# K leaves PSUM as one plain copy, its masked copies are made from SBUF, and the engine queues are ordered anew (two transformer layers, one core)

## The chip, the cores and the metric

One core of one Trainium2 chip runs the whole program. The engines are TensorE (PE, matmuls), VectorE (DVE), ScalarE (ACT), GpSimd (POOL) and SyncE (SP, which issues the DMAs here). Each works through its own queue in order; semaphores join them. The metric is the device time of one execution in microseconds, the median of several runs.

## The reference

Two times in a row, with the same weights, x becomes x plus attention of the normed x, and then x plus an MLP of the normed x. x has 2048 tokens of 512 features; there are 32 heads of 16; a token sees itself and the 255 tokens before it.

```python
def _layernorm(x, axis=-1, eps=1e-5):
    m = jnp.mean(x, axis=axis, keepdims=True)
    v = jnp.var(x, axis=axis, keepdims=True)
    return (x - m) / jnp.sqrt(v + eps)
...
    def _A_ref(x, wqkv, wo):
        B, S, D = x.shape
        H = 32; Dh = D // H; W = 256
        ...
        scores = jnp.einsum("bhqd,bhkd->bhqk", q, k) * (Dh ** -0.5)
        idx = jnp.arange(S)
        mask = (idx[:, None] - idx[None, :] >= 0) & (idx[:, None] - idx[None, :] < W)
        scores = jnp.where(mask[None, None], scores, -1e9)
        p = _softmax(scores, axis=-1)
        o = jnp.einsum("bhqk,bhkd->bhqd", p, v)
        return (lambda x, *d: x.transpose(*d))(o, 0, 2, 1, 3).reshape(B, S, D) @ wo
    def _B_ref(x, w1, b1, w2, b2):
        h = jnp.einsum("bsd,df->bsf", x, w1) + b1
        h = _gelu(h)
        return jnp.einsum("bsf,fd->bsd", h, w2) + b2
    x = A_x
    x = x + _A_ref(_layernorm(x, axis=-1), A_wqkv, A_wo)
    x = x + _B_ref(_layernorm(x, axis=-1), B_w1, B_b1, B_w2, B_b2)
    x = x + _A_ref(_layernorm(x, axis=-1), A_wqkv, A_wo)
    x = x + _B_ref(_layernorm(x, axis=-1), B_w1, B_b1, B_w2, B_b2)
```

## The kernel before

**Tiling.** x stays in SBUF as 16 tiles of 128 tokens. Attention goes in blocks of 256 tokens, 8 for each of the two layers, so blocks 0 to 15; the MLP goes in ten jobs of two or four tiles (`JOBS`). The program is written as if block followed block (`lnq`, `kv`, `attention`, `mlp`), and every instruction becomes a node of a plan.

**One block.** `layernorm` takes the statistics on DVE (line 618, 620), adds epsilon (L624, on POOL or DVE), raises to -1/2 on POOL (L630), and `transposed` writes the normed row on DVE (L640); a DMA transpose (L645) brings it into the layout for the projections. Only the four first tiles are transposed by PE instead (L652). `lnq` projects Q, two groups for a block, and copies each out of PSUM by `evac` on DVE (L607) or ACT (L609) into a ring `QT` of `QR` blocks. `kv` projects K, two groups, and V, two groups.

**K in two masked copies.** A chunk of 128 features holds 8 heads of 16. The scores of a pair of heads come out of one matmul of 32 rows: K is stored twice, once with the odd heads' rows set to zero and once with the even heads'. `parmask` holds the two columns of ones and zeros. Before, one DVE instruction reads a projection's bank and writes both (L700), broadcasting the bank over the two masks, 1024 elements a partition.

**Scores and PV.** `visit` makes 512 columns of scores in four banks (L767, "score group"), ACT takes exp of two banks at once into `E` (L774, 300 of them), masks of the window's edges are multiplied in place on DVE or POOL (L795). `pv` multiplies with V (L819, "PV group", two for a block), with a column of ones for the sum; the result is transposed on DVE (L828), divided (L832, L836), transposed back (L842) and projected by Wo. `Vs` is V with its halves swapped, made by DMA (L715). All projections, Wo and the MLP's matmuls are issued at line 666. In the MLP Gelu runs on ACT out of PSUM (L899) or, after a DVE copy with the bias (L891), out of SBUF (L894).

**What sets the order.** The plan is not followed in the order in which it is written. `_ORDER` lists all nodes in the order in which they are put into the engines' queues, `_ALT` the nodes that go to their second engine, `_BANKS` the PSUM banks, and `_TURNS` pairs of nodes that are kept apart by an additional wait. All four were found by a search offline and stand as numbers in the program. `_Sched` derives the semaphore waits from the names of what each node reads and writes.

## Time and profile before

| | |
|---|---|
| three runs | 440.96, 440.57, 442.94 us (median 440.96) |
| profiled execution, first to last instruction | 439.3 us; the time around it is not listed by itself, the median is 1.7 us above |
| instructions | 16863 |
| busy: PE, PEld, DVE, ACT, POOL | 415.7, 230.2, 335.9, 386.7, 209.1 us |
| granted TensorE clock | 1.000 |
| HBM read, written | 8.00 MB, 2.10 MB |

PE stands for matmuls, PEld for weight loads, which overlap with them. In the profile's rows a line number is that of the program, the shape is written out<-in, and behind the bar stand the busy time in us with the mean duration in ns, and the idle time of the engine just before, with the engine and line that ended it. Lines of helpers (607, 609 and 666 among them) serve several operations; the tile's name tells them apart.

### The profile page before, as it was taken

The page shows a single profiled execution, that of the slowest core. Times are in us where ns is not written, and L with a number is a line of the kernel's source. Part 1 is how long each engine was busy: PE and PEld are TensorE (multiplying, and loading weights), DVE is VectorE, ACT ScalarE, POOL GpSimd, SP SyncE. Part 2 cuts the span into 40 slices and gives each one's busy share as a digit, 9 for nine tenths or more (in the row PEclk, how much of TensorE's full clock was granted, in tenths as well). Part 3 has the DMA queues.
Part 4 walks back from the last instruction along what each step waited for, and adds up shares of the span by engine and source line. Part 5 has one row for each costly group of instructions (what it writes and reads, how often), then busy time and mean ns, then how long its engine had stood idle before and what let it go on. Part 6 is the DMA issues. An engine that isn't in the chain of part 4 may idle for free.

```text
span 439.3 us, 16863 instructions
## 1 busy us (share of the span) xinstructions
PE 415.7 (95%) x7497; PEld 230.2 (52%) x7571; DVE 335.9 (76%) x635; ACT 386.7 (88%) x458; POOL 209.1 (48%) x233
## 2 busy tenths in 40 slices
PE   8989999998699989999999999999999999999997
PEld 4555756645444554454454455455564554544663
DVE  5999878789867788976899687878877586655941
ACT  3999988999999899999999989998889989899533
POOL 3776262373655366731566344442443645735040
PEclk9999999999999999999999999999999999999999
DMA  8782912102200303222040111201222003003030
GB/s 245 200 199 52 223 32 52 38 13 49 56 3 13 52 4 44 34 34 44 9 92 5 25 27 28 52 1 28 51 52 50 1 16 90 14 0 76 3 107 25
DMA packets 49060, 23.51 MB, mean 54 GB/s; under 512 B 34268, under 2 KB 48988, under 8 KB 48988
## 3 DMA queue, kind: packets, MB, share of 16 engines
q1 hardware_dynamic: 48988, 22.43, 23.2%
q8 instruction: 60, 0.98, 0.9%
q14 instruction: 12, 0.10, 0.1%
HBM read 8.00 MB, written 2.10 MB: 23 GB/s over the span
## 4 chain that ended last, share of the span: by engine, by line
PE 78%; ACT 10%; DVE 4%; issue 2%; DMA 2%; POOL 1%; SPq 1%; POOLq 0%; DVEq 0%
PE ps L666 60%; ACT E L774 9%; PE ps L767 9%; PE ps L819 8%; DMA xnTB<-xn 1%; DVE OD L828 1%; POOL E L795 1%; DVE KT L700 1%; DMA X<-in_A_x_dram 1%; ACT Va L609 0%; SPq L645 0%; DVE X L911 0%; SPq L715 0%; DVE E L795 0%; PE ps L652 0%
## 5 line engine op out<-in xcount | busy, mean ns | idle before, releaser
L774 ACT ACTIVATE E<-ps 128x1024 bf16<-128x1024 f32 x300 | 284.1, 1040 | 22.9 <-PE ps L767 21.4
L795 POOL TENSOR_TENSOR E<-E,mask 128x512 bf16<-128x512 bf16 (+2 forms) x112 | 121.6, 1098 | 108.3 <-ACT E L774 45.4
L666 PE MATMUL ps<-W_sb,gT 128*128 128x512 bf16 x415 | 106.5, 380 | 3.3 <-issue 2.6
L666 PE MATMUL ps<-xnTB,W_sb 128*128 128x512 bf16 (+1 forms) x542 | 105.6, 335 | 3.2 <-issue 1.4
L666 PEld LDWEIGHTS ps<-xnTB,W_sb 128*128 128x128 bf16 x560 | 51.9, 98 | 43.7 <-issue 4.1
L666 PE MATMUL ps<-xnTA,Wqkv_sb 128*128 128x256 bf16 x512 | 70.6, 273 | 1.8 <-DVE OD L828 1.1
L767 PE MATMUL ps<-QT,KT 32*128 32x128 bf16 (+3 forms) x1920 | 60.7, 231 | 4.7 <-ACT E L774 1.8
L666 PEld LDWEIGHTS ps<-W_sb,gT 128*128 128x128 bf16 x448 | 39.4, 98 | 43.2 <-issue 3.4
L795 DVE TENSOR_TENSOR E<-E,mask 128x512 bf16<-128x512 bf16 (+2 forms) x124 | 51.2, 437 | 13.9 <-ACT E L774 6.8
L828 DVE STREAM_TRANSPOSE OD<-ps 128x1024 f32<-128x1024 f32 x32 | 40.0, 1249 | 25.3 <-PE ps L819 25.2
L666 PEld LDWEIGHTS ps<-xnTA,Wqkv_sb 128*128 128x128 bf16 x512 | 46.4, 98 | 21.7 <-issue 3.2
L767 PEld LDWEIGHTS ps<-QT,KT 32*128 32x128 bf16 x1920 | 28.5, 92 | 51.1 <-ACT E L774 30.7
L899 ACT ACTIVATE gT<-ps,b1T 128x512 bf16<-128x512 f32 (+1 forms) x80 | 43.6, 607 | 9.9 <-PE ps L666 9.7
L907 POOL TENSOR_TENSOR Xb<-X,b2all 128x512 f32<-128x512 bf16 x32 | 36.8, 1153 | 20.5 <-DVE X L911 11.5
L618 DVE BATCH_NORM_STATS2 stat<-X 128x6 f32<-128x512 bf16 x64 | 43.3, 684 | 2.7 <-DMA X<-in_A_x_dram 1.7
L819 PE MATMUL ps<-E,Va 64*17 64x256 bf16 (+3 forms) x1920 | 41.4, 230 | 3.0 <-ACT E L774 1.3
L700 DVE TENSOR_TENSOR KT<-ps,parmask 128x1024 bf16<-128x1024 f32 x32 | 38.7, 1211 | 5.4 <-PE ps L666 5.1
L819 PE MATMUL ps<-E,Vs 64*17 64x192 bf16 (+3 forms) x1920 | 42.3, 230 | 0.0
L891 DVE TENSOR_SCALAR gT<-ps,b1T 128x512 bf16<-128x512 f32 (+1 forms) x60 | 36.8, 630 | 6.1 <-PE ps L666 5.8
L836 POOL TENSOR_TENSOR Nb<-OD,Rc 128x512 bf16<-128x512 f32 x18 | 19.0, 1057 | 43.1 <-DVE Rc L832 29.0
L630 POOL TENSOR_TENSOR rstd<-rstd,mhalf 128x2 f32<-128x2 f32 (+1 forms) x33 | 24.3, 736 | 29.1 <-DVE rstd L624 27.4
L819 PEld LDWEIGHTS ps<-E,Va 64*17 64x17 bf16 x1920 | 29.3, 84 | 13.4 <-issue 7.6
(49 smaller groups left out, 359.8 us busy)
## 6 DMA issues: line engine op xcount, KB each, us to landing
Vs<-Va SPq DMA_DIRECT2D x64, 68.0 KB, 2.1
W_sb<-in_B_w_dram SPq DMA_DIRECT2D x4, 512.0 KB, 5.7
out_dram<-X SPq DMA_DIRECT2D x16, 128.0 KB, 1.9
X<-in_A_x_dram SPq DMA_DIRECT2D x3, 512.0 KB, 6.2
Wqkv_sb<-in_A_wqkv_dram SPq DMA_DIRECT2D x4, 256.0 KB, 5.1
W_sb<-in_B_w_dram SPq DMA_DIRECT2D x1, 768.0 KB
W_sb<-in_B_w_dram SPq DMA_DIRECT2D x2, 384.0 KB, 5.5
Wqkv_sb<-in_A_wqkv_dram SPq DMA_DIRECT2D x1, 512.0 KB, 6.2
```

The lines of the kernel that those rows point to most:

```text
L618: add("dve", lambda e, B, t=t, k6=k6: e.bn_stats(stat6[:, k6, :], X[:, t, :]), reads=["X%d" % t], writes=["st%d" % k6], key="bs%d" % (k + j))
L630: add("pool", lambda e, B, j=j, n=n: e.tensor_tensor(out=rstd[:, k + j : k + j + n], in0=rstd[:, k + j : k + j + n], in1=mhalf[:, 0:n], op ...
L666: r = e.matmul(ps[:, B[g][0], cols], lhsT, rhs, start=st, stop=sp)
L700: add("dve", lambda e, B, g=g, i=i: e.tensor_tensor(out=KT[:, kb, 2 * i : 2 * i + 2].rearrange("p c m a q -> p a (c m) q"), in0=ps[:, B[g] ...
L767: x = e.matmul(ps[:, bk[r], o : o + n], KT[rows, kb, c, m].rearrange("p a q -> p (a q)"), QT[rows, c, q : q + n], start=True, stop=True)
L774: add("act", lambda e, B, g_=g_, gi=gi: e.activation(E[:, 2 * gi : 2 * gi + 2, e0 : e0 + 512], ps[:, B[g_][0] : B[g_][0] + 2, :], AF.Exp, ...
L795: fn = lambda e, B: e.tensor_tensor(out=Ew, in0=Ew, in1=Mw, op=ALU.mult)
L819: x = e.matmul(ps[32 * r : 32 * r + VW, B[g][par], c % 2 * 2 * P + lo : c % 2 * 2 * P + hi], V[rows, (2 * b + m // 2) % VR, c * HC + 2 * r ...
L828: add("dve", lambda e, B: e.transpose(OD[:, s].rearrange("p a c q -> p (a c q)"), ps[:, B[g][0] : B[g][0] + 2, :]), reads=["ps:" + g], wri ...
L891: add("dve", lambda e, B, g=g, fc=fc: e.tensor_scalar(out=gT[:, fc, c0 : c0 + M], in0=ps[:, B[g][0], 0:M], scalar1=b1T[:, fc : fc + 1], sc ...
L899: add("act", lambda e, B, g=g, fc=fc: e.activation(gT[:, fc, c0 : c0 + M], ps[:, B[g][0], 0:M], AF.Gelu_apprx_tanh, bias=b1T[:, fc : fc + ...
L907: add("pool", lambda e, B, t=t, xs=xs: e.tensor_tensor(out=Xb[:, xs, :], in0=X[:, t, :], in1=b2all[:], op=ALU.add), reads=["X%d" % t, "b2a ...
```

## The change

K's projection leaves its bank by `evac`, as one plain copy on DVE or ACT, into `Kf`, a ring of two half blocks. Two `tensor_scalar` instructions, one for each column of `parmask`, write the two masked copies from there; each may stand on POOL or on DVE. The normed row of `transposed` may stand on POOL too. The ring of Q has four blocks instead of five. The four lists were searched anew with these choices.

```diff
-    QR = 5
+    QR = 4
+    NKF = 2
...
+        Kf = sb("Kf", [P, NKF, 8, HK])
...
-            add("dve", lambda e, B: e.tensor_scalar(
-                out=xn[:, s, :], in0=X[:, t, :], scalar1=statmv[:, k, 0:1], scalar2=rstd[:, k : k + 1],
-                op0=ALU.subtract, op1=ALU.mult),
-                reads=["X%d" % t, "mv%d" % k, "rs%d" % k], writes=["xn%d" % s], key="xn%d" % k)
+            def norm(e, B):
+                return e.tensor_scalar(
+                    out=xn[:, s, :], in0=X[:, t, :], scalar1=statmv[:, k, 0:1], scalar2=rstd[:, k : k + 1],
+                    op0=ALU.subtract, op1=ALU.mult)
+
+            add("dve", norm, reads=["X%d" % t, "mv%d" % k, "rs%d" % k], writes=["xn%d" % s], key="xn%d" % k,
+                alt=(("pool", norm),))
...
-                proj(g, 1, i, xs, xr, names)
-                add("dve", lambda e, B, g=g, i=i: e.tensor_tensor(
-                    out=KT[:, kb, 2 * i : 2 * i + 2].rearrange("p c m a q -> p a (c m) q"),
-                    in0=ps[:, B[g][0], :].rearrange("p (k q) -> p k q", q=HK)[:, None, :, :].to_broadcast([P, 2, 8, HK]),
-                    in1=parmask[:, :, None, None].to_broadcast([P, 2, 8, HK]), op=ALU.mult),
-                    reads=["ps:" + g, "parmask"], writes=names, free=[g], key="ke%d_%d" % (b, i))
+                proj(g, 1, i, xs, xr, [])
+                kf = (2 * b + i) % NKF
+                evac(lambda B, kf=kf: Kf[:, kf],
+                     lambda B, g=g: ps[:, B[g][0], :].rearrange("p (k q) -> p k q", q=HK),
+                     ["ps:" + g], ["KF%d" % kf], free=[g], key="ke%d_%d" % (b, i))
+
+                for a in range(2):
+                    def spread(e, B, i=i, kf=kf, a=a):
+                        return e.tensor_scalar(
+                            out=KT[:, kb, 2 * i : 2 * i + 2, :, a, :].rearrange("p c m q -> p (c m) q"), in0=Kf[:, kf],
+                            scalar1=parmask[:, a : a + 1], scalar2=None, op0=ALU.mult)
+
+                    add("pool", spread, reads=["KF%d" % kf, "parmask"], writes=[n + "ab"[a] for n in names],
+                        key="ks%d_%d_%d" % (b, i, a), alt=(("dve", spread),))
...
-                    rd += ["K%d_%d" % (kb, c), "Q%d_%d" % (b % QR, c)]
+                    rd += ["K%d_%da" % (kb, c), "K%d_%db" % (kb, c), "Q%d_%d" % (b % QR, c)]
```

The lists are too long to show; which engine they give the movable instructions to is this:

| instructions | before | after |
|---|---|---|
| K out of PSUM (32) | DVE 32, masked | DVE 25, ACT 7, plain |
| spreads of K (64) | none | POOL 37, DVE 27 |
| normed rows (64) | DVE 64 | POOL 43, DVE 21 |
| masks (236) | DVE 124, POOL 112 | DVE 141, POOL 95 |
| Q out of PSUM (32) | DVE 22, ACT 10 | DVE 24, ACT 8 |
| V out of PSUM (32) | DVE 15, ACT 17 | DVE 22, ACT 10 |
| additions of epsilon (33) | POOL 22, DVE 11 | POOL 18, DVE 15 |
| transposed rows out of PSUM (4) | ACT 3, DVE 1 | ACT 2, DVE 2 |

The order of the first DMAs changes as well. Before: X in three loads (4 tiles), weights of K and of Q (half each), X (4 tiles), then the rest of the weights. After: X in three loads, X (4 tiles), weights of K (second half), of Q (first half), of K (first half), of V.

## The prediction

> **What bounds the kernel now.** I read the page first (engine shares and the chain that ended last), then the windows, to see where the share of each engine changes, then the chain in order of time, the waits, and the groups with their shapes kept apart.

> ```profile
> PE 415.7 (95%) x7497; PEld 230.2 (52%) x7571; DVE 335.9 (76%) x635; ACT 386.7 (88%) x458; POOL 209.1 (48%) x233
> PE 78%; ACT 10%; DVE 4%; issue 2%; DMA 2%; POOL 1%; SPq 1%; POOLq 0%; DVEq 0%
> ```

> TensorE (PE) is busy 415.7 of 439.3 us, so at most 23.6 us can be won by feeding it better. ScalarE (ACT) at 88% is the second wall. The windows show that they take turns (columns: stretch, its length, then PE, PEld, DVE, ACT and POOL busy with instruction counts, granted clock, DMA share, GB/s):

> ```profile
> 10.00:40.00 30.00, 27.44 (x548) 16.88 (x552) 28.51 (x51) 27.61 (x33) 21.68 (x28) 1.00 0.66 167
> 40.00:80.00 40.00, 38.66 (x649) 26.61 (x651) 32.72 (x66) 37.04 (x52) 17.22 (x20) 1.00 0.43 91
> 80.00:120.00 40.00, 34.44 (x866) 19.02 (x871) 33.98 (x63) 39.30 (x47) 19.45 (x23) 1.00 0.22 43
> 120.00:160.00 40.00, 38.46 (x712) 19.85 (x717) 28.38 (x54) 37.24 (x43) 21.01 (x22) 1.00 0.11 19
> 160.00:200.00 40.00, 37.25 (x722) 20.30 (x730) 34.42 (x67) 37.96 (x44) 22.99 (x25) 1.00 0.25 34
> 200.00:240.00 40.00, 38.88 (x753) 19.77 (x760) 34.68 (x64) 37.93 (x43) 21.19 (x21) 1.00 0.18 38
> ```

> From 10 to 40 us VectorE (DVE) is at 28.51 of 30. From 80 to 120 us ACT is at 39.30 of 40, and there PE loses 5.6 us. From 120 to 200 us PE loses another 1.5 + 2.8 = 4.3 us, with ACT, DVE and PE all high. After 200 us PE loses about one us in forty. The chain says the same; its ACT link of 80 to 120 us and two PV groups (block 2's second one, and block 7's second one, which I use below as a milestone) are these:

> ```profile
> 81.51 1.57 PE ps L819 x96
> ...
> 107.61 12.83 ACT E L774 x14
> ...
> 211.10 1.30 PE ps L819 x96
> ```

> So the kernel's length is settled before about 211 us: how early ACT gets through its exps, and how seldom PE waits, up to that point. Behind it PE streams nearly without a gap, the same instructions in both kernels.

> **The change part by part.** The counts below are counted in the new lists of order and of alternatives. PE's instructions are the same ones. The prices:

> ```profile
> L700 DVE TENSOR_TENSOR KT<-ps,parmask 128x1024 bf16<-128x1024 f32 x32 | 38.7, 1211 | 5.4 <-PE ps L666 5.1
> L607 DVE CAST QT<-ps 128x512 bf16<-128x512 f32 x22 | 14.9, 676 | 0.4 <-PE ps L666 0.3
> L609 ACT ACTIVATE Va<-ps 128x512 bf16<-128x512 f32 x17 | 10.4, 614 | 0.7 <-PE ps L666 0.7
> L640 DVE TENSOR_SCALAR xn<-X,statmv,rstd 128x512 bf16<-128x512 bf16 x64 | 24.7, 401 | 12.1 <-POOL rstd L630 8.3 <-POOL Nb L836 2.3 <-POOL E L795 1.2
> L795 POOL TENSOR_TENSOR E<-E,mask 128x512 bf16<-128x512 bf16 x59 | 67.8, 1154 | 38.3 <-DVE Nb L836 12.6 <-ACT E L774 11.9 <-DVE E L795 7.9
> L795 POOL TENSOR_TENSOR E<-E,mask 128x256 bf16<-128x256 bf16 x33 | 21.9, 668 | 34.3 <-ACT E L774 24.3 <-DVE statmv L620 4.0 <-DVE xn L640 3.7
> L795 DVE TENSOR_TENSOR E<-E,mask 128x512 bf16<-128x512 bf16 x57 | 23.2, 414 | 5.0 <-POOL E L795 2.6 <-ACT E L774 1.6 <-POOL Xb L907 0.6
> L795 DVE TENSOR_TENSOR E<-E,mask 128x256 bf16<-128x256 bf16 x23 | 6.5, 281 | 3.3 <-POOL E L795 2.6 <-POOL Nb L836 0.6 <-ACT E L774 0.2
> L624 POOL TENSOR_SCALAR rstd<-statmv 128x2 f32<-128x2 f32 x21 | 5.2, 248 | 10.9 <-DVE statmv L620 10.8
> L624 DVE TENSOR_SCALAR rstd<-statmv 128x2 f32<-128x2 f32 x10 | 1.7, 168 | 0.3
> L553 POOL TENSOR_SCALAR mask<-mask 128x128 bf16<-128x128 bf16 x1 | 0.3, 298 | 0.1
> L607 DVE COPY xnTA<-ps 128x512 bf16<-128x512 bf16 x1 | 0.4, 424 | 0.7 <-PE ps L652 0.7
> ```

> *K's way out of PSUM.* The 32 masked copies at 1.211 us go (-38.7 us of DVE). In their place stand 32 plain copies of the shape that Q has: 25 on DVE at 0.676 (+16.9), 7 on ACT at 0.614 (+4.3 of ACT). Each bank comes free 0.53 to 0.60 us earlier. Who waited for the old instruction, from the view of its line:

> ```profile
> L700 DVE TENSOR_TENSOR KT<-ps,parmask x32: 1158/1219/1226, 10.2 to 352.1; 128x1024 bf16<-128x1024 f32 x32
> ...
> who waited for it (us, times):
>   PEld ps L666: 0.8, 2
> ```

> So the earlier bank is worth at most about 0.8 us, and I put it at nothing; with the cover of the other banks gone it would be 32 x 0.53 = 17 us.

> *The two spreads per copy,* 64 of 128x512 from SBUF: 27 on DVE, 37 on POOL. Neither is in the trace. On DVE the nearest row is the normed row at 0.401 (the same form: one tensor, one scalar per partition); the ends are 0.168 (two elements) and 0.676 (from PSUM). I take 0.401: +10.8, with ends of 4.5 and 18.3. On POOL two TENSOR_SCALAR rows, 248 ns for 2 elements and 298 ns for 128, give 0.4 ns an element and 0.45 us for 512; the two-input mask costs 1.154. I take 0.6, nearer to the row of the same operation. K is needed late: in both orders 12 us or more of PE work stand between a K projection and the first scores that read it, except for K of block 0 and the first half of block 1 at the start, where it is 2 to 3 us. So the added latency (copy, then spread: 0.68 + 0.6 against 1.21) is hidden everywhere but there. The ring of two buffers for the copy makes a K copy wait for the spreads two copies back; behind that copy on DVE or ACT stand masks and exps. With half blocks 10 us apart the cover is large.

> *Normed rows:* 43 of 64 go to POOL: -43 x 0.401 = -17.2 of DVE, +25.8 of POOL at 0.6 (19 to 50). The hop from POOL's power to DVE, for which DVE sat idle 8.3 us in all, goes where both stand on POOL; but DMA transposes on SP's queue now wait for POOL. By the orders, 6 us or more of PE work lie between the statistics and the first use, and this is as in the old order.

> *Placement anew:* 17 masks go from POOL to DVE (13 of 512, 4 of 256; 768 unchanged): DVE +13 x 0.414 + 4 x 0.281 = +6.5; POOL -13 x 1.154 - 4 x 0.668 = -17.7. Q copies: 2 more on DVE (+1.4); V copies: 7 more on DVE (+4.7); one transposed row more on DVE (+0.4); 4 additions of epsilon from POOL to DVE (+0.7, -1.0).

> *Sums.* DVE: -38.7 + 16.9 + 10.8 - 17.2 + 6.5 + 1.4 + 4.7 + 0.4 + 0.7 = -14.5, so 321 us (73%). POOL: 37 x 0.6 + 43 x 0.6 - 17.7 - 1.0 = +29.3, so 238 us (54%); by 0.45 an operation 226, by 1.154 283 us (64%). ACT: 7 K copies come, 2 Q, 7 V and 1 transposed row go: 3 copies fewer, -1.8 us. PE: 0. *Q's ring of four:* a block's Q is written before the block two behind is done, so four slots bind nobody; 0.

> *What of this lies on the path.* Only what lets ACT and PE reach the milestone sooner. Counting both orders up to that PV group of block 7, PE has exactly the same instructions before it (84 Q and 84 K parts, 168 and 154 MLP parts, 79 score groups, 15 PV groups), and ACT the same 157 exps and 44 Gelus; but 18 copies stand before it on ACT in the old order (5 Q, 3 transposed, 10 V), 15 in the new (5 K, 3 Q, 2 transposed, 5 V). At block 6's first PV group the counts are 17 against 13. In the stretch where ACT is at 39.30 of 40 a copy less is 0.6 us less: -1.8 us at the milestone (-2.4 at block 6). DVE's 14.5 us I put at nothing: its waits are 4% of the chain.

> *The start* costs something. Before the first score group the new order puts 12 K, 4 Q and 8 V parts, the old one 5 K and 8 Q:

> ```profile
> 7.42 0.60 ACT L609 ACTIVATE xnTA<-ps 128x512 bf16<-128x512 bf16 x1 [0.15 <-PE ps L652]
> 8.09 1.26 PE L666 MATMUL ps<-xnTA,Wqkv_sb 128*128 128x256 bf16 x10
> 11.74 0.40 PE L767 MATMUL ps<-QT,KT 32*128 32x256 bf16 x8
> 12.34 1.94 ACT L774 ACTIVATE E<-ps 128x1024 bf16<-128x1024 f32 x2
> 155.71 1.91 PE L666 MATMUL ps<-xnTA,Wqkv_sb 128*128 128x256 bf16 x16
> 4.00:6.00 2.00, 1.69 (x4) 0.30 (x2) 1.78 (x6) 0.00 (x0) 1.29 (x3) 1.00 0.98 276
> ```

> A projection matmul of 256 columns takes (1.91 - 0.27) / 15 = 0.109 us in a stream. Counted in those, 48 against 26 stand there: 2.4 us more, so the first exp comes at about 14.7 instead of 12.34 us; ACT has by then 2 copies more behind it (1.2 us), so it is 1.2 us behind, PE not at all. Part of it is lost again anyhow between 40 and 80 us, where ACT has 3 us of idle time. I take +0.4, between 0 and 1.2.

> Sum: -1.8 + 0.4 = -1.4 us. The profiled execution's span is 439.3, 1.3 below the lowest and 1.7 below the median of the three runs; I carry the difference over: span 437.9, time 440.96 - 1.4 = 439.6 us. Half a per cent (2.2 us) is about what a measurement of this kernel can tell from no change, so the forecast by itself is "no change", on the fast side.

> **The rivals.**

> *More is won: DVE's relief counts.* Up to the milestone DVE has about 6 us less work in its queue by the prices above (21 masked copies against 16 plain ones and 17 spreads, 38 normed rows against 11, some 22 masks and copies more), and masks move from 1.15 us on POOL to 0.41 on DVE ahead of PV groups. PE's 4.3 us of idle time between 120 and 200 us then shrink. Half of it gone: 440.96 - 1.8 - 2.1 = 437.1; all of it: 434.9. For it: all three queues are in order and DVE is above 85% busy from 160 to 240 us. Against it: PE's direct waits for DVE are small.

> *Slower: POOL becomes late.* Between the PV group of 81 us and the milestone 28 spreads and normed rows come onto POOL, whose masks gate PV groups, and 6 masks leave it (about 6.6 us). From 80 to 200 us POOL was busy 19.45 + 21.01 + 22.99 = 63.5 us, 53%; that becomes about 74 us (61%) at 0.6 an operation and 89 (74%) at 1.154, in order, with operations that wait for ACT in between. If each of the 10 PV groups there waits for one POOL operation more (0.6) with PE standing: +6, so 440.96 - 1.4 + 6 = 445.6. It decides from about 0.8 us for a POOL spread or normed row on. For it: POOL's idle time is mostly waiting, which can't be used at will. Against it: the order moves 17 masks off POOL.

> *The weights come late at the start.* The new order loads four more tiles of X (0.5 MB) ahead of every weight; at 276 GB/s that is 1.9 us. Before, the first projection began at 8.09, just after the copy from 7.42 to 8.02, so how long the weights had been there isn't shown. All 1.9 lost: 441.5; nothing lost is the forecast.

> *DVE and POOL block each other.*

> ```profile
> L640 DVE TENSOR_SCALAR xn<-X,statmv,rstd x64: 314/408/415, 5.6 to 419.0; 128x512 bf16<-128x512 bf16 x64
> L795 DVE TENSOR_TENSOR E<-E,mask x124: 229/420/561, 21.4 to 408.6; 128x512 bf16<-128x512 bf16 x57, 128x768 bf16<-128x768 bf16 x44, 128x256 bf16<-128x256 bf16 x23
> L795 POOL TENSOR_TENSOR E<-E,mask x112: 663/1152/1643, 16.6 to 403.6; 128x512 bf16<-128x512 bf16 x59, 128x256 bf16<-128x256 bf16 x33, 128x768 bf16<-128x768 bf16 x20
> ```

> If a DVE operation on SBUF waited for a running POOL operation, 188 such (124 masks, 64 normed rows) before and 189 (141, 27, 21) after would each wait half an operation with POOL's share as the chance; a share that rises from 48 to 54% adds 189 x 0.06 x 0.5 = 5.7 us to DVE, and if half of that is passed on to PE the time is 442.4. The rows speak against it: with POOL busy half the time no normed row took over 415 ns (minimum 314), no mask over 561. [...]

> **How the numbers follow.** Forecast 0.38 (439.6; own range 437.5 to 441.5), DVE's relief 0.25 (437.1), POOL late 0.23 (445.6), weights late 0.10 (441.5), blocking 0.04 (442.4). Faster by over 0.5% (below 438.8): 0.24 of the relief and 0.15 of the forecast: 0.39. Slower (above 443.2): 0.22 of POOL late, 0.02 of the forecast, 0.05 of the last two, whose prices have ends above that: 0.29. The rest, 0.32, is within. The range runs from the relief's far end to POOL late's value, 434.9 to 445.6, rounded outward a little at the top; each side leaves out about one in ten.

> **What would show it.** Right: spreads on POOL near 0.6 us and on DVE near 0.4; POOL near 238, DVE near 321, ACT near 385 us busy; the PV group of block 7 that began at 211 us begins near 209.6 and the same lead is there at the end; ACT in 80 to 120 us still above 39 of 40. Wrong: PE's waits for POOL's masks growing by microseconds (POOL late); PE idle in 120 to 200 us clearly below 4.3 (relief); the first projection after 9 us (weights late); normed rows or masks on DVE at two or three times their present maximum (blocking).

## The result: 523.1 us, 18.6% slower

The changed kernel takes 523.07 us (median of 520.6 to 524.87), the kernel before on the same chip 440.76 (439.64 to 442.94): a ratio of 1.186, 95% interval 1.1823 to 1.1898. The profiled execution's span is 519.8 us against 439.3. The page of the changed kernel, busy times and the shares of the chain that ended last:

```profile
PE 431.1 (83%) x7499; PEld 236.2 (45%) x7571; DVE 319.1 (61%) x643; ACT 387.6 (75%) x455; POOL 335.8 (65%) x292
...
POOL 41%; PE 25%; DVE 21%; ACT 4%; issue 4%; DMA 3%; DVEq 0%; SPq 0%; POOLq 0%
```

DVE and ACT came out near the forecast (321 and 385). GpSimd has 335.8 us in place of 238, and the chain, 78% PE before, is now 41% GpSimd. PE's own 15 us more are the same instructions at a lower granted clock (0.964 on average), as the windows show (stretch, length, busy PE, PEld, DVE, ACT, POOL with counts, granted clock, DMA share, GB/s):

```profile
10.00:40.00 30.00, 20.82 (x307) 12.54 (x311) 16.75 (x40) 19.34 (x23) 21.91 (x19) 0.89 0.59 161
40.00:80.00 40.00, 30.81 (x575) 19.45 (x560) 25.70 (x51) 27.77 (x37) 27.14 (x22) 0.91 0.28 70
80.00:120.00 40.00, 30.07 (x554) 19.14 (x559) 22.63 (x49) 29.66 (x38) 26.98 (x22) 0.96 0.15 32
120.00:160.00 40.00, 27.91 (x662) 16.01 (x666) 25.16 (x50) 27.91 (x31) 30.00 (x24) 0.89 0.17 36
```

No engine is full in any of them: DVE at 28.51 of 30 and ACT at 39.30 of 40 are gone, and nothing took their place. That is the picture of engines that wait for each other in turn. GpSimd's groups and the waits (engine and line that wait, who released them, us in all, times, longest) say for whom:

```profile
L649 POOL TENSOR_SCALAR xn<-X,statmv,rstd 128x512 bf16<-128x512 bf16 x43 | 89.3, 2078 | 7.4 <-DVE E L814 4.7 <-DVE xn L649 0.6 <-DVE KT L718 0.5
L718 POOL TENSOR_SCALAR KT<-Kf,parmask 128x512 bf16<-128x512 bf16 x37 | 58.1, 1573 | 28.2 <-DVE E L814 15.8 <-DVE Kf L615 6.5 <-DVE KT L718 1.8
L814 POOL TENSOR_TENSOR E<-E,mask 128x512 bf16<-128x512 bf16 x46 | 52.9, 1154 | 23.9 <-DVE E L814 19.8 <-ACT E L793 1.9 <-DVE xn L649 1.5
```

```profile
ACT E L793 <- PE ps L786: 84.2, 64, 4.8
POOL E L814 <- DVE E L814: 48.5, 26, 9.0
DVE E L814 <- POOL xn L649: 25.7, 9, 4.1
```

A normed row costs GpSimd 2.08 us and a spread 1.57, both far above the 0.6 that I took and above the upper end of 1.154. 43 x 1.48 + 37 x 0.97 = 99.5 us, which accounts for the surplus of 97.8. And GpSimd's masks wait 48.5 us for DVE's masks (25.1 before), DVE's masks 25.7 us for normed rows on GpSimd. A mask does not read a normed row: these are the turns, the additional waits of `_TURNS`. The chain in order of time (start, length, what) shows one:

```profile
134.67 0.73 POOL rstd L638
...
135.50 4.15 POOL xn L649 x2
...
139.74 0.70 DVE Nb L855
...
140.52 0.70 POOL rstd L638
141.22 1.12 POOL E L814
```

DVE's `Nb` of a PV group stands until two rows on GpSimd are through, and GpSimd's next operations stand until `Nb` is.

### The profile page after: what moved, and what is told of

Same layout as the page of the kernel before. It is cut to its first block, busy times and chain, and to the rows that moved or that the text cites. A ratio compares the mean times of both kernels' runs of the same rounds, so it can differ in the third digit from the quotient of the medians.

```text
span 519.8 us, 16941 instructions
## 1 busy us (share of the span) xinstructions
PE 431.1 (83%) x7499; PEld 236.2 (45%) x7571; DVE 319.1 (61%) x643; ACT 387.6 (75%) x455; POOL 335.8 (65%) x292
## 3 DMA queue, kind: packets, MB, share of 16 engines
q1 hardware_dynamic: 48988, 22.43, 18.6%
## 4 chain that ended last, share of the span: by engine, by line
POOL 41%; PE 25%; DVE 21%; ACT 4%; issue 4%; DMA 3%; DVEq 0%; SPq 0%; POOLq 0%
PE ps L677 18%; POOL xn L649 15%; POOL KT L718 10%; POOL E L814 9%; DVE E L814 7%; ACT E L793 4%; POOL rstd L638 4%; PE ps L838 3%; PE ps L786 3%; DMA xnTB<-xn 3%; POOL Xb L926 2%; DVE OD L847 2%; POOL Nb L855 2%; DVE gT L910 1%; DVE stat L626 1%
## 5 line engine op out<-in xcount | busy, mean ns | idle before, releaser
L814 POOL TENSOR_TENSOR E<-E,mask 128x512 bf16<-128x512 bf16 (+2 forms) x95 | 104.3, 1108 | 56.8 <-DVE E L814 48.5
L677 PE MATMUL ps<-xnTB,W_sb 128*128 128x512 bf16 (+1 forms) x543 | 108.2, 343 | 12.1 <-DVE gT L910 4.2
L677 PE MATMUL ps<-W_sb,gT 128*128 128x512 bf16 x416 | 108.6, 387 | 6.0 <-issue 3.3
L814 DVE TENSOR_TENSOR E<-E,mask 128x512 bf16<-128x512 bf16 (+2 forms) x141 | 57.6, 435 | 68.9 <-POOL xn L649 25.7
L649 POOL TENSOR_SCALAR xn<-X,statmv,rstd 128x512 bf16<-128x512 bf16 x43 | 89.3, 2078 | 7.4 <-DVE E L814 4.7
L786 PE MATMUL ps<-QT,KT 32*128 32x128 bf16 (+3 forms) x1920 | 62.9, 236 | 24.8 <-issue 6.5
L677 PE MATMUL ps<-xnTA,Wqkv_sb 128*128 128x256 bf16 x512 | 72.2, 283 | 6.6 <-DVE X L930 3.2
L718 POOL TENSOR_SCALAR KT<-Kf,parmask 128x512 bf16<-128x512 bf16 x37 | 58.1, 1573 | 28.2 <-DVE E L814 15.8
L838 PE MATMUL ps<-E,Va 64*17 64x64 bf16 (+3 forms) x1920 | 42.7, 237 | 23.5 <-DVE E L814 10.8
L677 PEld LDWEIGHTS ps<-xnTA,Wqkv_sb 128*128 128x128 bf16 x512 | 48.7, 101 | 27.1 <-issue 7.4
L847 DVE STREAM_TRANSPOSE OD<-ps 128x1024 f32<-128x1024 f32 x32 | 39.7, 1241 | 14.9 <-PE ps L838 14.9
```

The lines of the kernel that those rows point to most:

```text
L649: return e.tensor_scalar(out=xn[:, s, :], in0=X[:, t, :], scalar1=statmv[:, k, 0:1], scalar2=rstd[:, k : k + 1], op0=ALU.subtract, op1=ALU ...
L677: r = e.matmul(ps[:, B[g][0], cols], lhsT, rhs, start=st, stop=sp)
L718: return e.tensor_scalar(out=KT[:, kb, 2 * i : 2 * i + 2, :, a, :].rearrange("p c m q -> p (c m) q"), in0=Kf[:, kf], scalar1=parmask[:, a ...
L786: x = e.matmul(ps[:, bk[r], o : o + n], KT[rows, kb, c, m].rearrange("p a q -> p (a q)"), QT[rows, c, q : q + n], start=True, stop=True)
L814: fn = lambda e, B: e.tensor_tensor(out=Ew, in0=Ew, in1=Mw, op=ALU.mult)
L838: x = e.matmul(ps[32 * r : 32 * r + VW, B[g][par], c % 2 * 2 * P + lo : c % 2 * 2 * P + hi], V[rows, (2 * b + m // 2) % VR, c * HC + 2 * r ...
```

## The experiments

Times are medians, beside runs of the kernel before on the same chip (440.3 to 441.4). "Rows" are the normed rows, "spreads" K's masked copies.

**Which of the two moves costs.** The changed kernel, with rows, spreads or both kept on DVE:

```diff
         for i in _ALT:
-            nodes[i]["eng"], nodes[i]["fn"] = nodes[i]["alts"][1]
+            if not nodes[i]["key"].startswith("xn"):      # rows stay on DVE
+                nodes[i]["eng"], nodes[i]["fn"] = nodes[i]["alts"][1]
+        for nd in nodes:                                  # spreads go to DVE
+            if nd["key"].startswith("ks"):
+                nd["eng"], nd["fn"] = nd["alts"][1]
```

> The new order with all 64 normed rows and all 64 spreads on DVE, nothing else changed. Theory P (price): the loss comes from what one-input operations cost on POOL, 2.08 us for a normed row and 1.57 us for a spread where 0.6 was forecast, so that POOL, 336 us busy, runs behind the order that was searched for it. Then here POOL falls to about 188 us, DVE rises by 43 x 0.41 + 37 x 0.35 = 31 to about 350 us, and the time is 438 to 455 us. Theory O (order): the new order, its banks, the ring of two for the plain copy or Q's ring of four are bad by themselves. Then it stays above 490 us whoever makes the rows and spreads.

> The new order with the normed rows on DVE; the 37 spreads stay on POOL. POOL loses 89 us (to about 247), DVE gains 18 (to about 337). Theory P by load: most of the loss goes, 445 to 465 us, since POOL is then as busy as the forecast had it (238). If the spreads on POOL are what hurts (K late, the ring of two buffers held), it stays above 480. Theory O: above 490.

> The new order with the spreads on DVE; the 43 normed rows stay on POOL. POOL loses 58 us (to about 278), DVE gains 13 (to about 332). Theory P by load: a good third of the loss goes, 475 to 500 us, because rows are the larger part of POOL's excess and stand in a chain (statistics, row, transpose, projection). If spreads are what hurts: below 460. Theory O: above 490.

Measured: both on DVE 455.84 us (ratio 1.0335, 1.0318 to 1.0352), just above the range of theory P; only the spreads on GpSimd 462.66 (1.0435 to 1.0553); only the rows 486.54 (1.1014 to 1.1058). So having the rows and spreads on GpSimd accounts for 67 of the 82 us, and the two do not add up: spreads alone cost 6.8, rows alone 30.7, both 67.2. The other 15 us stay when both are on DVE.

**Price or place.** GpSimd's 43 rows, and its spreads behind block 4 (24 of the 37; the first five blocks' spreads are whole, on DVE), do only part of the 512 columns; the other columns are left out.

```diff
+            def part(e, B):
+                return e.tensor_scalar(
+                    out=xn[:, s, 0:D//4], in0=X[:, t, 0:D//4], ...)
-                alt=(("pool", norm),))
+                alt=(("pool", part),))
```

> The new order with rows and spreads on POOL as they are, but each of POOL's rows and spreads handles only 128 of its 512 columns (the rest keeps what an earlier tile left; the output is not the reference's). The spreads of blocks 0 to 4 stand on DVE at full width, 24 narrow ones stay on POOL. By 0.22 us plus 3.6 or 2.6 ns an element these cost about 0.68 and 0.56 us: the price of the forecast. Theory P: the time is that of the forecast, 436 to 446 us, and PE's clock is granted in full. Theory O: above 490 us.

> As the run with a quarter of the columns, with 256 of the 512 columns done on GpSimd (the others left out): a masked copy 0.92 us by the run of GpSimd's prices, a normed row about 1.2, between 0.79 for 128 columns and 2.07 for 512. If the time grows in proportion to GpSimd's work, the line from the quarter (0.80 and 0.61, 451.7 us) to the full width (2.08 and 1.57, 523 us with all 37 copies) gives 470 to 476 us; if GpSimd has slack up to a threshold near 1 us and costs only beyond it, 452 to 460 us.

> The changed kernel, in which GpSimd's 43 normed rows and its masked copies of K behind the fifth block (24) work on 8 of the 512 columns only, some 0.25 us each by the small rows of the page (248 ns for two columns); the rest of those columns is left out, and the masked copies of the first five blocks are made whole on the vector engine. With a quarter of the columns (0.80 and 0.61 us) the time was 451.7. Theory F (what is left above the kernel before is the new order's own, from blocks of TensorE's instructions that run through faster than the next is fetched): GpSimd's share is gone already at 0.8 us, and the time is 447 to 452 us. Theory P (GpSimd is late even at 0.8 us, and nothing else is): the 36 us taken off GpSimd bring the time down to 439 to 443 us.

| columns | row, spread on GpSimd (us) | GpSimd busy (us) | time (us) |
|---|---|---|---|
| 8 | 0.40, 0.31 | 213.9 | 449.48 (ratio 1.0189 to 1.0266) |
| 128 | 0.80, 0.61 | 237.5 | 451.72 (1.0226 to 1.0263) |
| 256 | 1.22, 0.93 | 263.3 | 463.34 (1.0505 to 1.0553) |
| 512, the changed kernel | 2.08, 1.57 | 335.8 | 523.07 |

The time for eight columns lies in the range of theory F, the quarter is above its theory P (436 to 446), and the half lies between its two ranges. The quarter is by chance the case that I had forecast: 237.5 us of GpSimd (forecast 238), 323.4 of DVE (321). It stands 11 us above the kernel before, and above the forecast's upper end of 446.0, so the price was not the only step that failed. The first 24 us of GpSimd's work cost 2 us, the next 26 cost 12, the last 72 (13 more spreads among them) 60. 71 of the 82 us are the price beyond the quarter; some 9 to 11 stay when GpSimd is hardly busier than before (213.9 us against 209.1).

**The price by itself.** The kernel before, and behind its last output, with all other engines idle, eleven forms five times each on GpSimd (one execution).

```diff
+            lambda e, B: e.tensor_scalar(out=KD, in0=src8, scalar1=pm, scalar2=None, op0=ALU.mult),
+            lambda e, B: e.tensor_tensor(out=KD, in0=src8, in1=col[:, :, None].to_broadcast([P, 8, HK]), op=ALU.mult),
+            lambda e, B: e.tensor_copy(dst, src),
...
```

> The kernel before, and behind its last output 55 operations on GpSimd alone, five of each of eleven forms, while every other engine is idle. Theory A, the price is GpSimd's own: the form of the spread (one multiply by a pointer, 512 columns, written to K's interleaved places) takes about 1.57 us and the form of a normed row (subtract and multiply by two pointers) about 2.08 us, as in the kernel after, within 3%; with constants in place of the pointers each comes to about the same, so that the second arithmetic step, not the pointer, makes the 0.5 us between them; a row of 128 columns costs about 0.8 us. [...] Theory C, the strided write is what costs: the spread form written to plain places comes under 1.0 us. The two-input multiply by a mask that is already known from the two-input masks is about 1.15 us per 512 columns by all of them.

Its GpSimd groups from 440 us on (busy, mean ns of one | idle before); the eleventh form, the spread's with a constant to plain places, ran just ahead of them. L943 is the row's form with constants, L944 the spread's written to plain places, L945 the row, L946 the spread with a constant, L947 the spread, L948 a two-input multiply by the mask's column, L950 to L952 narrower:

```profile
L945 POOL TENSOR_SCALAR xn<-gT,statmv,rstd 128x512 bf16<-128x512 bf16 x5 | 10.4, 2072 | 0.5
L944 POOL TENSOR_SCALAR xn<-gT,parmask 128x512 bf16<-128x512 bf16 x5 | 7.8, 1562 | 0.5
L947 POOL TENSOR_SCALAR KT<-gT,parmask 128x512 bf16<-128x512 bf16 x5 | 7.8, 1560 | 0.5
L946 POOL TENSOR_SCALAR KT<-gT 128x512 bf16<-128x512 bf16 x5 | 7.4, 1489 | 0.4
L943 POOL TENSOR_SCALAR xn<-gT 128x512 bf16<-128x512 bf16 x3 | 5.8, 1922 | 0.2
L948 POOL TENSOR_TENSOR KT<-gT,mask 128x512 bf16<-128x512 bf16 x5 | 5.2, 1040 | 0.4
L950 POOL TENSOR_SCALAR xn<-gT,parmask 128x256 bf16<-128x256 bf16 x5 | 4.6, 922 | 0.5
L952 POOL TENSOR_SCALAR xn<-gT,statmv,rstd 128x128 bf16<-128x128 bf16 x5 | 4.0, 792 | 0.5
L949 POOL COPY xn<-gT 128x512 bf16<-128x512 bf16 x5 | 3.1, 613 | 0.3
L951 POOL TENSOR_SCALAR xn<-gT,parmask 128x128 bf16<-128x128 bf16 x5 | 3.0, 602 | 0.5
```

The two prices are GpSimd's own, with nobody beside it. The strided write costs nothing (1560 against 1562), a pointer in place of a constant 70 ns (two pointers 150), the second arithmetic step 0.4 to 0.5 us. The one-step form is (1562 - 602) / 384 = 2.5 ns a column and 0.28 us, the two-step form 3.3 and 0.37. A two-input multiply is cheaper than the one-input one (1.04 against 1.56), and only the plain copy has the price that I had given to all, 0.6.

**The cheaper form.** The changed kernel with rows on DVE and the spreads as two-input multiplies:

```diff
-                        return e.tensor_scalar(out=..., in0=Kf[:, kf], scalar1=parmask[:, a : a + 1], ...)
+                        return e.tensor_tensor(out=..., in0=Kf[:, kf],
+                            in1=parmask[:, a : a + 1, None].to_broadcast([P, 8, HK]), op=ALU.mult)
```

> The changed kernel with the normed rows on the vector engine and the masked copies of K written as a two-input multiply by the mask's column in bf16, 37 of them on GpSimd: 1.04 us each by the run of GpSimd's prices, in place of 1.57, so 19.6 us less on GpSimd than in the run that keeps the rows on the vector engine (462.7). Theory A (it is the price per copy that costs): the time falls below 462.7, to 453 to 458 us, toward the 455.8 with everything on the vector engine. Rival (what costs is that the scores wait for another engine at all, at whatever price): 461 to 464 us.

458.05 us (454.76 to 459.42; ratio 1.0407 to 1.0452) against 462.66 with 1.57 us. That points to the price per copy but does not show it: 4.6 us is little more than the spread of the runs, and DVE's 27 spreads changed too (0.69 us instead of 0.35).

**What is left when GpSimd is cheap.** In all kernels with the new order PE stops for up to 2.5 us in the middle of groups of short matmuls with nothing to wait for ("issue"). The kernel before's page lists an instruction queue with 60 packets, of 16384 bytes each in the trace (0.98 MB):

```profile
q8 instruction: 60, 0.98, 0.9%
```

That is one for every 256 of PE's some 15,300 instructions. To see whether the stops are the fetch of the next 256, the kernel before got an instruction stream that is shifted by 64 places: seven of the eighteen warming matmuls at its start became 39 of one column.

```diff
+        drop = [i for i, nd in enumerate(PL.nodes) if nd["key"] in ["warm%d" % h for h in range(3, 10)]]
+        for h in range(39):   # weights and one column: two instructions each
+            add("pe", lambda e, B, bk=h % 8: e.matmul(ps[:, bk, 0:1], gT[:, 0, 0:P], gT[:, 0, 0:1], ...
```

> The kernel before with seven of the eighteen warming matmuls at its start replaced by 39 of a single column, so that every later instruction of TensorE stands 64 places further on (a matmul and its weight load are one each); nothing else differs. Theory F, TensorE stalls of 1 to 2 us appear where a 16384-byte block of its instructions is run through faster than the next one can be fetched: the new places of the block boundaries put about a dozen of them into groups of short matmuls, and the time is 447 to 453 us, with the stalls spaced by about 255 instructions. Theory G, the stalls of the new order have another cause (a dependency, an engine that is late): the time stays at 440 to 442 us and no stall over 0.7 us appears in the middle of a group of short matmuls beyond the one at 159.85 us.

> The changed kernel with normed rows and masked copies all on the vector engine (455.8 us), with four of the eighteen warming matmuls left out, so that every later instruction of TensorE stands 8 places earlier. Theory F (block boundaries of the instruction fetch): the five stalls of 0.7 to 2 us move away from their places in the instruction stream, some vanish, others appear; the time changes by 1 to 6 us, down to about 450 us if the blocks that now run through in about 3.1 us become longer. Theory G: the stalls stay at the same instructions with the same lengths, and the time stays within 1 us of 455.8.

> The run with eight columns, with eight of the eighteen warming matmuls replaced by 46 of a single column, so that every later instruction of TensorE stands 76 places further on; the same columns are left out. Theory F: the stalls sit at other places of the work but at the same places of the instruction stream (193 more than a multiple of 256, as in the shifted kernel before and in the run with 8 instructions less), there are more of them, and the time rises by 12 to 25 us above that of the eight columns. Theory G (stalls from dependencies of the order): the same time within 1.5 us.

The shifted kernel before takes 471.26 us (ratio 1.0646 to 1.072): 30 us for 64 places. The "issue" pieces above 0.6 us of its chain (start, length in us), where the kernel before has none:

```profile
38.28 2.62 issue
122.58 2.69 issue
185.38 2.42 issue
201.82 1.95 issue
248.94 0.98 issue
266.42 1.81 issue
316.68 1.85 issue
401.51 0.63 issue
406.32 1.99 issue
440.39 1.37 issue
```

Counting PE's recorded matmuls, weight loads and semaphore instructions in order of time, the nine stops above 0.9 us stand before numbers 1217, 4289, 6593, 7105, 8641, 9153, 10689, 14017 and 15041: each 193 more than a multiple of 256. In the run with 8 instructions less (454.56 us, 1.3 under its unshifted form) the five stops above 0.6 us stand at 1217, 1729, 2753, 4289 and 10689, again 193 more than a multiple of 256, so they stayed at their places in the stream and moved by 8 instructions in the work. In the other runs some matmul records are missing; counted by weight loads, the stops of all kernels with the new order stand there too, in the changed kernel itself before 1217, 1729, 2753 and 4289 (5.1 us). The eight columns in two alignments, as they are and 76 places on:

```profile
41.13 2.04 issue
56.47 1.50 issue
85.15 0.97 issue
124.60 1.24 issue
```

```profile
102.91 2.31 issue
150.08 1.26 issue
178.09 2.10 issue
235.11 1.82 issue
281.63 0.70 issue
324.77 1.70 issue
338.62 1.63 issue
386.11 2.24 issue
```

5.8 us of stops became 13.8, and the time went from 449.48 to 456.55 (two runs, 454.11 and 458.98): 8.0 us more stops, 7.1 us more time by the medians and 5.4 between the two executions shown. In the packets' times of the shifted kernel, the fetch at eight of the nine places starts 0.85 to 2.0 us after PE enters a block and takes 1.0 to 1.6; at the ninth (14017) it starts only 3.84 us after and takes 0.9. At all nine PE goes on 1.2 to 1.6 us after the packet has landed. So in the shifted kernel a block of short matmuls that PE ran through in less than some 3.5 us was mostly followed by a stop: 13 of the 15 such blocks were, and the other two had their fetch begin within 0.2 us. The kernel before has no such stop above 0.6 us in its alignment; the new order has three to eight in each that was run. My expectation of 447 to 453 us for the shifted kernel before was far too low, and that of 12 to 25 us for the shift by 76 too high. Of the 30 us, 18.3 are the stops listed; the rest (a mean granted clock of 0.978 in place of 1.000, engines that run late behind a stop) was not split further.

**The same moves in the order before.** First the 43 rows alone on GpSimd, then K's split alone on DVE (copy, odd half from it, even half in place), then with GpSimd's two-input form from block 5 on, directly behind the copy and 30 or 60 operations later.

```diff
-            add("dve", ...                                  # the row
+            add("pool" if k in POOL_ROWS else "dve", norm, ...
```

```diff
+                add("dve", lambda e, B, ...: e.tensor_copy(half[0], ps[:, B[g][0], :]...), free=[g], ...)
+                for a in (1, 0):                            # first "dve"; then "pool", two-input
+                    add("dve", lambda e, B, ...: e.tensor_scalar(out=half[a], in0=half[0], scalar1=parmask[:, a : a + 1], ...
```

> The kernel before with one thing changed: the same 43 normed rows as in the change are made by GpSimd, at 2.08 us instead of 0.41 us on the vector engine; K stays as it was. In the new order the same rows alone (masked copies on the vector engine) stood 30.7 us above the kernel with everything on the vector engine. Theory A (the price is what costs, in either order, because the masks of the scores queue behind the rows on GpSimd): 462 to 478 us. Rival (the new order was laid out for cheap rows and only it is hurt; in the old order TensorE's queue covers them): 443 to 455 us.

> The kernel before, its order and its Q ring of five, with K's step alone split in three on the vector engine: a plain copy from PSUM into the even half of K's place, the odd half made from it, the even half masked in place. 32 groups: the copy 0.68, the two masked copies 0.35 each by the rows of the kernel with both on the vector engine, so 1.38 instead of 1.21 us, 5.3 us more work on the vector engine. Theory 1, the split itself is cheap and the loss lies in GpSimd's prices and in the new order of the engines' work: 440 to 445 us. Theory 2, the split lengthens the path from a K projection to the scores and so accounts for most of the 15 us by which the new order with everything on the vector engine stood above the kernel before: 448 to 456 us.

> The kernel before, its order of the engines' work and its Q ring of five; from the fifth block on (b from 5, 22 of the 32 groups) K leaves PSUM as one plain copy of 0.68 us on the vector engine, and GpSimd makes the two masked halves with the two-input multiply of 1.04 us, the second in place; the first five blocks stay as they were. The vector engine is relieved by 22 x 0.53 = 11.7 us, GpSimd takes 44 x 1.04 = 45.8 us more (209 to 255). TensorE's instructions keep their places. Theory A (the idea of the change holds where GpSimd's price is near 1 us and no stall of the instruction fetch comes with it): 438 to 442 us. Rival (GpSimd's own masks of the scores and the scores that wait for K come later by the 2.1 us of each group's pair, whatever the price): 444 to 452 us, with TensorE's and GpSimd's waits for each other growing behind 100 us.

> As the run of the order before with GpSimd's two-input copies of K (480.7), with each pair of masked copies placed 30 operations further on in the order of all engines' work (2963 operations in 439 us, so some 4 us), still well ahead of the first scores that read them (83 to 425 operations). GpSimd's work is the same 255 us. Theory Q (the 40 us came from the place: GpSimd, which works in order, stood at each pair until the vector engine had copied, 29.2 us of waits, and its score masks stood behind): 440 to 448 us, with GpSimd's waits for the copy under 5 us. Rival P (the 45.8 us of work itself, wherever it stands, makes the score masks late): 465 us or more.

> The same with 60 operations in place of 30. Theory Q: 438 to 446 us; if the wait was the whole cost, nothing is gained over 30. Rival P: 465 us or more. Under 439 us it would beat the kernel before.

Rows: 471.14 us (ratio 1.0671 to 1.0727), 30.9 above the kernel before, in the new order 30.7. The same rows cost the same in both, with turns laid for them and without. The split on DVE: 454.16 (1.0272 to 1.0325), although PE's instructions have their places of before. Its spreads in the view of their line (ns: minimum, median, maximum):

```profile
L709 DVE TENSOR_SCALAR KT<-KT,parmask x64: 352/354/1610, 10.6 to 367.2; 128x512 bf16<-128x512 bf16 x64
```

The median is the price that I had expected, but their mean in the groups is 556 ns: 64 x 0.20 = 12.9 us more, about the loss of 13.3. The time lies in the range of theory 2, but whether the longer path has a part in it was not tried.

The split with GpSimd: 480.73 us directly behind the copy, far above both ranges, 459.9 and 458.9 further on. In the first GpSimd waits 29.2 us for the copies (us in all, times, longest):

```profile
POOL KT L716 <- DVE KT L712: 29.2, 13, 7.9
```

Moving the pairs wins back 21 us. But 18 remain, more than the one theory had and less than the other. These pairs have no turns; with 30 operations, 37 of DVE's 124 masks overlap GpSimd's work and single ones take up to 1.39 us, which leads to the last question.

**What holds an operation of 0.35 us for 1.6?** In the runs that moved work without new turns, single rows, masks and spreads on DVE took 1.0 to 1.8 us; in the two kernels themselves none took over 0.63. So both kernels without turns:

```diff
-        for a, z in zip(_TURNS[0::2], _TURNS[1::2]):
+        for a, z in ():
```

> The kernel before without its 182 turns, the extra semaphore waits that let an operation of the vector engine and one of GpSimd on SBUF begin only when the other engine's has ended; everything else, the order of each engine's own work included, is the same (TensorE's instructions move by one place at most). Theory L (an operation of these forms that meets a running one of the other engine is held until that ends, and the turns hide it): without turns normed rows and masks on the vector engine overlap GpSimd's work in the records and reach 1.0 to 1.8 us in place of at most 0.415 and 0.561, as some did in the runs that moved work between the engines without new turns; the time is 440 to 455 us. Theory N (the engines do not hinder each other; the long durations of those runs had another cause): maxima as before, and the time stays or falls, 436 to 441 us.

> The changed kernel without its 187 turns, else the same (TensorE's instructions move by at most eight places). The turns make its vector engine and GpSimd take SBUF by turns: 335.8 us of GpSimd and some 80 us of masks, rows, masked copies and Nb of the vector engine stand one after the other, 416 of 519.8 us. Theory L (held operations and waits for turns are the same exclusion paid in two ways): the vector engine's busy time grows by 20 us or more, its masks and rows reach 2 us, and the time stays high, 495 to 530 us. Theory N (the waits for turns alone made GpSimd's price so dear): the time falls to 460 to 485 us with the vector engine still near 319 us busy.

Before without turns: 453.76 us (ratio 1.0262 to 1.0296). The changed kernel without turns: 479.38 us (1.0812 to 1.0881), 44 us faster than with them. The pages, the kernel before first, each with DVE's rows or masks without turns:

```profile
PE 418.5 (93%) x7497; PEld 230.2 (51%) x7571; DVE 365.6 (81%) x635; ACT 387.7 (86%) x458; POOL 213.9 (47%) x233
```

```profile
L640 DVE TENSOR_SCALAR xn<-X,statmv,rstd x64: 313/408/1666, 5.4 to 432.9; 128x512 bf16<-128x512 bf16 x64
L795 DVE TENSOR_TENSOR E<-E,mask x124: 228/426/1872, 21.9 to 421.6; 128x512 bf16<-128x512 bf16 x57, 128x768 bf16<-128x768 bf16 x44, 128x256 bf16<-128x256 bf16 x23
```

```profile
PE 418.6 (88%) x7499; PEld 232.2 (49%) x7571; DVE 355.5 (75%) x643; ACT 386.1 (81%) x455; POOL 348.1 (73%) x292
```

```profile
L814 DVE TENSOR_TENSOR E<-E,mask x141: 252/520/1978, 23.8 to 444.1; 128x512 bf16<-128x512 bf16 x70, 128x768 bf16<-128x768 bf16 x44, 128x256 bf16<-128x256 bf16 x27
```

In the kernel before DVE's same instructions take 29.7 us longer (335.9 to 365.6), rows up to 1.67 us and masks up to 1.87, where with turns no row took over 0.415 and no mask over 0.561. In the records, DVE's rows overlap an operation of GpSimd in 3 of 64 cases with turns and in 32 without; in 28 of the 32 GpSimd had begun first, and the row ends 0.15 us (median) after GpSimd's operation. Statistics overlap GpSimd in 45 of 64 cases of the kernel before, and with or without turns none takes over 0.696. `Nb` on DVE takes up to 1.64 us without turns in both kernels (0.693 with them), a spread in the changed kernel up to 1.22 (0.354), and a row on GpSimd there up to 2.89 (2.09). So in these two runs DVE's rows, masks, spreads and `Nb` and GpSimd's operations held each other up when they met; statistics were not held. My reading in the prediction, that rows of at most 415 ns and masks of at most 561 speak against blocking, was wrong: the turns had already taken most of these overlaps out of the trace that I read (masks overlap in 17 of 124 cases with turns, 48 without).

In the changed kernel the turns cost more than the blocking that they avoid: without them 12 us more on GpSimd and 36 on DVE still leave it 44 us ahead. Neither theory for that run holds whole: the time lies in N's range, DVE's growth and the mask of 1.98 us are L's. The likely reason, which is argued and not shown: the turns fix which operation goes first, and the 187 orders were found for operations of other lengths than these.

## Why the prediction was wrong, point by point

The forecast was 439.6 us with 434.9 to 446.0; measured were 523.1.

*The step that failed first: the price of a one-input operation on GpSimd.* I took 0.6 us from rows of 2 and 128 columns and gave 1.154, the two-input mask, as the upper end. Measured 2.08 and 1.57; beyond the price of the quarter (0.80 and 0.61) that is worth 71 of the 82 us. The row of 298 ns for 128 columns (L553) misled me: the same engine takes 602 to 792 ns for 128 columns of the forms in question (that row has constants in place of pointers and reads 64 columns twice; why it is short was not tried). An end "from the nearest row" was no end, because I supposed that one input costs less than two.

*The rival that came true in kind: GpSimd late.* It put the turning point at about 0.8 us. The runs put the bend between 0.8 and 1.2: 449.5 us at 0.40 and 0.31, 451.7 at 0.80 and 0.61, 463.3 at 1.22 and 0.93. Its size was off, since it priced one operation of waiting at each of ten PV groups (+6) and no more.

*The second step that failed: blocking.* I gave it 0.04 because no duration was long. The 5.7 us of waiting on DVE was my estimate from the busy shares, and no run shows it; without turns DVE's busy time was 29.7 us longer in the kernel before and 36 in the changed one. Blocking is a large part of why GpSimd's work is so dear: taking the turns alone out won back 44 us (a share that overlaps with the 71). DVE's forms that were held without turns are 87.5 us before (rows 24.7, masks 23.2 + 6.5 and, for 768 columns, 23.5, `Nb` 9.6); with GpSimd's 209.1 that makes 297 of 439 us. Nearly as many stand in the changed kernel (87), and with 335.8 they make 422 of 520 us, nearly all one after the other (one of these 203 DVE operations overlaps GpSimd in the changed kernel). GpSimd's 65% of the span and these forms of DVE together are 81% of it. I read the turns in the program and costed neither them nor what they hide.

*What I put at nothing: the order's own cost.* "PE's instructions are the same ones" is true, but which of them share a block of 256 changed, and that brought 5.8 us of stops (eight columns). With these stops taken off, the eight columns stand at about 443.7, 3 us above the kernel before. That rest is not settled: the rings of four and of two, the order of the first loads and the turns were not run alone in it.

*The milestone.* Block 7's second PV group begins at 263.1 us instead of 211.0, and the stretch behind it grew from 228.3 to 256.7: it does not stream without a gap when GpSimd's masks are late.

*Right:* DVE's sum, and ACT's within 1% (387.6 against 385, though it did not fall); DVE's spread (0.347 against 0.401), copies of 0.683 and 0.613; the first projection at 8.00 us, so the weights came in time. No run shows a gain from *DVE's relief*.

No kernel here beats the one before; the nearest is the eight columns, which leaves work out.

## What to carry to other kernels

Price an operation that moves to GpSimd by that very form at that very size: a copy of 512 columns took 0.61 us, a two-input multiply 1.04, a multiply by a scalar 1.56 and a subtract-multiply 2.08. A trace whose program keeps two engines apart by waits can't tell that they would not hinder each other, so add up the work of both that must go in turn and compare that sum with the span. A new order of short matmuls also moves the ends of PE's blocks of 256 instructions; in the kernel before, 64 places were worth 30 us.
